# Weights' sign in a Prelu, sums of squares as 128x32 tiles, loads in pairs of chunks: one change to a chunked scan with two gated MLPs

## The chip, the core and the metric

The kernel runs on one core of a Trainium2 chip. A core has TensorE (PE; its weight loads are listed as PEld), VectorE (DVE), ScalarE (ACT), GpSimd (POOL) and SyncE (SP, which issues transfers); each takes its own instructions in order, and they meet at semaphores. The metric is the time of one execution on the device in microseconds (us).

## The reference, cut to what matters

Three stages follow each other. The first is a decayed linear attention over chunks (4 batches, 8 heads, 768 positions, head size 32, state size 16), the second a gated MLP behind an RMS norm, the third an MLP with a hard gate.

```python
# per chunk of 32 positions, per batch and head
cum = np.cumsum(log(clip(a)))
M = (C @ B.T) * exp(cum[:, None] - cum[None, :]) * causal
y = M @ x + (C @ state) * exp(cum)[:, None]
state = exp(sum(la)) * state + (B * exp(cum[-1] - cum)[:, None]).T @ x
# 3072 tokens, width 256 = heads x head size
xn = x / sqrt(mean(x * x) + 1e-6) * rms_g
x = (silu(xn @ w_gate) * (xn @ w_val)) @ w_out      # d_ff 1536
h = x @ w_in                                        # d_ff 2048
out = (h * clip(h + 3, 0, 6) / 6) @ w_out2
```

The weights arrive as 64-bit floats and are turned into 32-bit ones on the chip; the other inputs are 32-bit.

## The kernel before, in words

**Tiling.** The 24 attention chunks (6 blocks of 128 positions by 4 batches, all heads together; `k` counts them) are worked two at a time. For a chunk the kernel loads `cb` (B, C and x in three layouts, 448 KB), `L` (the decay factors of 64 positions, broadcast to the partitions, 256 KB in two transfers) and `P` (prefix products, 64 KB). A scan on VectorE turns `L` into decays, PE makes scores (L395) and state terms (L406), VectorE multiplies by the decays (`SM`, L449), and PE adds the parts within (L420) and from the state (L429). Four chunks make a block of 512 tokens. ScalarE squares them (`sq`), and `norm` (L581) sums the squares over the width, takes 1/sqrt by a bit trick and three Newton steps on VectorE (L519 to L521), writes the 512 results to DRAM (`rnd`, L601), reads them back broadcast to 128 partitions (`rb`, L605), and scales the block with them (L609). The first block has its own form, `norm_pair` (L526), which goes over PE instead of DRAM.

**The MLPs.** The first MLP ("A") takes 6 blocks by 12 slices `f` of d_ff; a step is two hidden products of 6 matmuls each and one output product of 6 (every product in three parts, high and low halves of both operands, `mm3`, L716). The second ("B") takes 6 blocks by 16 slices, with 6 and 6 matmuls. A step goes PE, ScalarE (gate `p`, L751 or L753), VectorE (product `p`, L759 or L761), ScalarE (`gh`), VectorE or GpSimd (`gl`), PE. Only two buffers hold hidden products of A, so PE cannot go far ahead of the product `p` on VectorE.

**Weights.** For each slice, `weights` (L648) loads 64-bit words, ScalarE scales the high words by a Copy (`high`, L664) and the low words (`low`, L668), VectorE joins them by a shift and an or (`join`, L672) and puts the sign bit in (`sign`, L677), and two more operations split the result into high and low halves. There are 12 slices for A and 16 for B.

**What sets the order.** A list scheduler in Python, `Plan` (L38), gets every operation with an estimated cost, its inputs and outputs and a priority, simulates the engines, and writes the instructions in the order in which its simulation starts them. `visit` puts two attention chunks between MLP steps, at slices AT = [1, 5] of every block of A, and `norm` of the next block stands at slice AT_NORM = 7. All transfers are issued by SyncE in the order of the plan. After the last attention chunk, at `open2`, the buffers of the attention are given back and the weights of B are prepared.

Of the kernel before, what the change touches and what calls it, by code (L numbers as in the profile page):

```python
# [17 lines left out]
CH = 128  # L18
# [10 lines left out]
RAW = [17500, 12000]  # L29
BOOST = 6000  # L30
PACE = 0.9
AT = [1, 5]
AT_NORM = 7
NL = 3
NCB = 4


class Plan:  # L38
# [10 lines left out]
    LAT = {"PE": 250, "ACT": 150, "DVE": 130, "POOL": 150, "DMA": 2000, "HOST": 0}  # L49

    def __init__(self, bufs):
        self.bufs, self.ops = bufs, []
        self.last, self.readers, self.users, self.first = {}, {}, {}, {}
        self.fill, self.pace = None, {}

    def op(self, ns, fn, r=(), w=(), boost=0):

        i, deps, order = len(self.ops), set(), set()
        for k in r:
            deps.add(self.last[k])  # L60
        for k in w:
# [19 lines left out]
    def run(self):  # L81
# [8 lines left out]
        for i in reversed(range(len(ops))):  # L90
            ns = ops[i][0]
            e = min(ns, key=ns.get)
            tail[i] = ns[e] + max((tail[s] + (self.LAT[e] if full else 0)
# [9 lines left out]
        done, left, out = set(), set(), []  # L103

# [7 lines left out]
        while len(out) < len(ops):  # L112
# [39 lines left out]
            free[e] = end  # L152
            out.append((t, i, e))
            for s, full in succ[i]:
                ready[s] = max(ready[s], end + self.LAT[e] if full else t)
                wait[s] -= 1
                if wait[s] == 0:
                    enter(s)
# [18 lines left out]
def block_kernel(ctx, tc, comb, ablk, w1, w2, cst, out):  # L177
# [18 lines left out]
    ap3 = att.enter_context(tc.tile_pool(name="ap3", bufs=NL))  # L196
    apc = att.enter_context(tc.tile_pool(name="apc", bufs=NCB))
# [4 lines left out]
    ones = ap1.tile([128, 1], F32, name="ones")  # L202
# [5 lines left out]
    P = Plan({"L": NL, "cb": NCB, "P": NCB, "ch": 4, "bh": 2, "SM": 4, "um": 4, "V": 6, "V1": 4,  # L208
# [9 lines left out]
    def dma(nbytes):  # L218
        return {"DMA": max(500, nbytes // 300)}
# [4 lines left out]
    def d1(n):  # L224
        return 65 + 1.05 * n
# [26 lines left out]
    def setup():  # L252
# [3 lines left out]
        act.activation(out=spare, in_=half, func=AF.Sqrt)  # L256
# [15 lines left out]
    rnd = dram.tile([NB, B * CH], F32, name="rnd")  # L272
# [16 lines left out]
    def put_pref(e):  # L289
        for c in range(2):  # L290
            nc.sync.dma_start(
                out=pref.rearrange("k (q g c i) -> c (k q) g i", q=2, c=2, i=SC)[c],
                in_=ac[48 * c:48 * c + 48])

    def prefixes():
        P.op(dma(98304), lambda e: nc.sync.dma_start(out=ac, in_=rows(ablk)), w=[("ac", 0)],
             boost=1e5)
        P.op({"DVE": d2(256) + 200}, clip_all, r=[("ac", 0), ("eye", 0)], w=[("az", 0)], boost=1e5)
        P.op({"DVE": ds(256)}, prefix, r=[("az", 0)], w=[("ac", 0)], boost=1e5)
        P.op(dma(98304), put_pref, r=[("ac", 0)], w=[("pref", 0)], boost=1e5)  # L300
        P.op(dma(98304), lambda e: nc.sync.dma_start(out=gs, in_=cst), w=[("cs", 0)], boost=2e4)
        P.op(dma(98304), lambda e: nc.sync.dma_start(out=rows(azero), in_=az), r=[("az", 0)],
             w=[("azero", 0)], boost=2e5)

# [25 lines left out]
    def load(k):  # L330
        bst = BOOST if k >= B else BOOST0 + (3000 if k < 2 else 0)

        def ld_cb(e, a, b):
            if ("cb", k) not in T:
                T["cb", k] = apc.tile([128, CW], F32, tag="cb", name="cb")
            nc.sync.dma_start(out=T["cb", k][:, a:b], in_=comb[k][:, a:b])

        def ld_L(e):
            T["L", k] = t = ap3.tile([128, H, SC], F32, tag="L", name="L")
            src = azero if k else ablk  # L340
            for c in range(2):
                nc.sync.dma_start(out=flat(t[64 * c:64 * c + 64]),
                                  in_=src[c, k].partition_broadcast(SC))

        def ld_P(e):
            T["P", k] = t = apc.tile([128, CH], F32, tag="P", name="P")
            src = pref[k].rearrange("(h n i) -> h n i", n=1, i=CH).to_broadcast([H, N, CH])
            nc.sync.dma_start(out=t, in_=src)

        def clip(e):  # L350
            t = T["L", k]
            eng[e].tensor_scalar(out=t, in0=t, scalar1=1e-6, scalar2=1.0, op0=ALU.max, op1=ALU.min)
            eng[e].memset(t[:, :, 0:1], 0.0)

        if k == 0:
            P.op(dma(262144), ld_L, w=[("L", k)], boost=1e5)
            prefixes()
            P.op({"DVE": d1(512)}, clip, r=[("L", k)], w=[("L", k)], boost=bst)
        else:
            P.op(dma(262144), ld_L, r=[("azero", 0)], w=[("L", k)], boost=bst)  # L360
        if k < B:
            P.op(dma(262144), lambda e: ld_cb(e, 0, XX), w=[("cb", k, 0)], boost=bst)
            P.op(dma(196608), lambda e: ld_cb(e, XX, CW), w=[("cb", k, 1)], boost=bst)
        else:
            P.op(dma(458752), lambda e: ld_cb(e, 0, CW), w=[("cb", k, 0), ("cb", k, 1)], boost=bst)
        P.op(dma(65536), ld_P, r=[("pref", 0)], w=[("P", k)], boost=bst)


        def scan(e):
# [4 lines left out]
        P.op({"DVE": ds(512)}, scan, r=[("eye", 0), ("L", k)], w=[("L", k)], boost=bst)  # L374

        def ch(e):
# [4 lines left out]
        def bh(e):  # L381
# [4 lines left out]
        P.op(either(128), bh, r=[("cb", k, 1), ("L", k)], w=[("bh", k)], boost=bst)  # L386
# [566 lines left out]
```

## Time and profile before

| | us |
|---|---|
| median of 3 runs | 711.05 (709.69 to 711.46) |
| the profiled execution: its own time | 709.71 |
| the profiled execution: its span | 707.9 |
| PE busy | 627.9 (89% of the span) |
| VectorE busy | 328.4 (46%) |
| ScalarE busy | 292.9 (41%) |
| GpSimd busy | 263.7 (37%) |
| first matmul of the MLP starts at | 36.68 |
| last instruction's chain: PE on lines 718 | 35% and 26% of the span |
| the same chain: DMA `rnd`, DMA `rb` | 7% and 3% of the span |

PE's busy share is high, but its records overlap, so the share alone doesn't tell how near PE is to its rate; the spacing of the matmuls does. The span begins and ends with stretches in which PE waits or does small work, and between them lie five waits of several us that the timeline of PE shows by themselves. From about 411 us on, PE works without a gap to the end.

### The profile page before, as it was taken

How to read it: one execution, taken by the hardware profiler on the slowest of the kernel's cores; microseconds unless marked ns; L12 is line 12 of the kernel's file. 1: busy time of each engine (PE TensorE's matmuls, PEld its weight loads, DVE VectorE, ACT ScalarE, POOL GpSimd, SP SyncE). 2: the span in 40 equal slices, each digit the busy share in tenths (PEclk: the TensorE clock that was granted, in tenths of full speed). 3: DMA queues.
4: the chain of work that ended last, by engine and by line, in shares of the span. 5: the costliest groups of instructions: out<-in, count | busy, mean ns of one | idle time of the engine just before them, and what ended most of it. 6: DMA issues, size and time to landing. Idle time of an engine off the chain costs nothing.

```text
span 707.9 us, 10946 instructions
## 1 busy us (share of the span) xinstructions
PE 627.9 (89%) x4414; PEld 508.5 (72%) x4414; DVE 328.4 (46%) x518; ACT 292.9 (41%) x483; POOL 263.7 (37%) x228
## 2 busy tenths in 40 slices
PE   2587968994999499959779999999999999999997
PEld 1465757783878387748668778888888888888886
DVE  4699956562156215523258894232233322332323
ACT  1465623321332133223145663545545445454453
POOL 2155423221332122212123434555455545554443
PEclk9998988998999799979979999999999999999999
DMA  7916711230023004100132430000000000000000
GB/s 204 353 62 196 260 20 38 91 91 15 1 91 90 16 0 118 42 15 2 10 125 97 143 120 0 1 1 0 31 1 30 1 0 31 1 30 1 18 12 30
DMA packets 21089, 42.18 MB, mean 60 GB/s; under 512 B 5360, under 2 KB 9136, under 8 KB 21040
## 3 DMA queue, kind: packets, MB, share of 16 engines
q1 hardware_dynamic: 21040, 41.50, 18.7%
q8 instruction: 34, 0.56, 0.4%
q14 instruction: 15, 0.12, 0.1%
HBM read 38.14 MB, written 3.35 MB: 59 GB/s over the span
## 4 chain that ended last, share of the span: by engine, by line
PE 65%; DMA 12%; DVE 10%; issue 5%; ACT 2%; POOL 1%; SPq 0%; DVEq 0%; POOLq 0%; ACTq 0%
PE hps L718 35%; PE acc L718 26%; DMA rnd<-y 7%; DMA rb<-rnd 3%; DMA L<-azero 2%; DVE p L759 1%; DVE cv L677 1%; PE sps L429 1%; PE sps L420 1%; DVE cv L672 1%; DVE z L520 1%; ACT p L751 1%; DVE L L371 1%; DVE gl L240 1%; DVE xT L609 1%
## 5 line engine op out<-in xcount | busy, mean ns | idle before, releaser
L240 POOL TENSOR_TENSOR gl<-p,gh 128x512 fp32r<-128x512 f32 x150 | 196.9, 1313 | 283.2 <-ACT gh L766 274.4
L766 ACT CAST gh<-p 128x512 fp32r<-128x512 f32 x168 | 104.6, 623 | 118.9 <-PE acc L718 116.8
L761 DVE SCALAR_TENSOR_TENSOR p<-p,hps 128x512 f32<-128x512 f32 x96 | 65.9, 687 | 171.3 <-ACT p L753 171.2
L718 PE MATMUL hps<-xh,w1h 128*128 128x512 f32 x288 | 97.6, 421 | 53.6 <-DVE p L759 42.4
L718 PEld LDWEIGHTS hps<-xh,w1h 128*128 128x128 f32 x288 | 54.3, 198 | 71.6 <-DVE p L759 46.5
L753 ACT ACTIVATE p<-hps,half 128x512 f32<-128x512 f32 x96 | 66.0, 688 | 81.5 <-POOL gl L240 80.5
L718 PE MATMUL hps<-xh,w1l 128*128 128x512 f32 x288 | 93.1, 406 | 0.9 <-POOL w1l L240 0.9
L718 PE MATMUL hps<-xl,w1h 128*128 128x512 f32 x288 | 92.8, 405 | 0.0
L759 DVE TENSOR_TENSOR p<-p,hps 128x512 f32<-128x512 f32 x72 | 49.0, 681 | 65.4 <-PE hps L718 60.9
L751 ACT ACTIVATE p<-hps 128x512 f32<-128x512 f32 x72 | 43.0, 597 | 80.7 <-POOL gl L240 54.8
L718 PE MATMUL acc<-gl,w2h 128*128 128x512 f32 x192 | 74.7, 389 | 0.0
L718 PE MATMUL acc<-gh,w2h 128*128 128x512 f32 x192 | 74.7, 389 | 0.0
L718 PE MATMUL acc<-gh,w2l 128*128 128x512 f32 x192 | 74.7, 389 | 0.0
L718 PEld LDWEIGHTS hps<-xh,w1l 128*128 128x128 f32 x288 | 56.8, 197 | 14.0 <-POOL w1l L240 1.3
L718 PEld LDWEIGHTS hps<-xl,w1h 128*128 128x128 f32 x288 | 56.6, 197 | 12.6
L718 PE MATMUL hps<-xl,w2h 128*128 128x512 f32 x192 | 59.1, 389 | 0.0
L718 PE MATMUL hps<-xh,w2h 128*128 128x512 f32 x192 | 59.1, 389 | 0.0
L718 PE MATMUL hps<-xh,w2l 128*128 128x512 f32 x192 | 59.1, 389 | 0.0
L718 PE MATMUL acc<-gh,w1h 128*128 128x512 f32 x144 | 57.6, 400 | 0.0
L718 PE MATMUL acc<-gh,w1l 128*128 128x512 f32 x144 | 56.9, 395 | 0.0
L718 PE MATMUL acc<-gl,w1h 128*128 128x512 f32 x144 | 56.6, 393 | 0.0
L718 PEld LDWEIGHTS acc<-gh,w2l 128*128 128x128 f32 x192 | 36.1, 188 | 7.5
(99 smaller groups left out, 748.3 us busy)
## 6 DMA issues: line engine op xcount, KB each, us to landing
cb<-comb SPq DMA_DIRECT2D x20, 448.0 KB
raw<-w SPq DMA_DIRECT2D x16, 512.0 KB
L<-azero SPq DMA_DIRECT2D x46, 128.0 KB
yT<-w SPq DMA_DIRECT2D x6, 768.0 KB
rawx<-w SPq DMA_DIRECT2D x6, 768.0 KB
out<-yT SPq DMA_DIRECT2D x12, 256.0 KB
P<-pref SPq DMA_DIRECT2D x24, 64.0 KB
rb<-rnd SPq DMA_DIRECT2D x5, 256.0 KB
```

The lines of the kernel that those rows point to most:

```text
L240: eng[e].tensor_tensor(out=out, in0=a, in1=b, op=op)
L371: dve.tensor_tensor_scan(out=L, data0=L, data1=flat(eye8), initial=0.0, op0=ALU.mult, op1=ALU.add)
L420: pe.matmul(out=y[32 * g:32 * g + 32, 2 * t + c], rhs=SM[r, h], lhsT=cb[r, XX + D * h:XX + D * h + D], start=first, stop=True, skip_group_ ...
L429: pe.matmul(out=y[q:q + 64, p // 2 * 2 + c], lhsT=before(k, c)[r, :], rhs=T["ch", k][r, SC * c:SC * c + SC], start=False, stop=True, skip_ ...
L520: dve.tensor_tensor(out=z, in0=z, in1=y, op=ALU.mult)
L609: dve.scalar_tensor_tensor(out=x, in0=x, scalar=gs[:, t:t + 1], in1=T["rb", j], op0=ALU.mult, op1=ALU.mult)
L718: pe.matmul(out=o, lhsT=a, rhs=c, start=first and i == 0, stop=last and i == len(seq) - 1)
L751: act.activation(out=p[:, :n], in_=hid(hs[0])[:, :n], func=AF.Silu)
L753: act.activation(out=p[:, :n], in_=hid(hs[0])[:, :n], func=AF.Relu, scale=1.0 / 6.0, bias=half)
L759: dve.tensor_tensor(out=p, in0=p, in1=h, op=ALU.mult)
L761: dve.scalar_tensor_tensor(out=p, in0=p, scalar=1.0, in1=h, op0=ALU.min, op1=ALU.mult)
L766: act.copy(out=t[:, :n], in_=T["p", i][:, :n])
```

## The change

The diff does five things.

1. **Sign.** `high` uses Prelu with scale 2^-112 and alpha -2^32 in place of Copy. A negative word comes out positive with an exponent that is 32 higher, and the shift by 3 in `join` carries that bit into the sign. `sign` (28 VectorE operations, 12 of 128x768 and 16 of 128x512) is gone.
2. **Norm.** For the blocks 1 to 5 the sums of squares are made with a 128x32 tile of ones as the stationary operand, so that each batch's sums lie along 128 columns, repeated on 32 partitions. The VectorE chain (shift, guess, 3 Newton steps, 12 operations) works on 128x128 elements instead of 128x4. `rnd` is written by 4 transfers of one row of 128 numbers each; it was one transfer that took 4 numbers from each of 128 partitions.
3. **Loads in pairs.** `L`, `cb` and `P` are tiles of two chunks, two such tiles each (before: 3, 4 and 4 tiles of one chunk). A pair's `cb` is one transfer, from the second pair on, and a pair's `L` two transfers with 4 KB rows.
4. **ScalarE issues** the first two pairs' `cb` and the constants `gs`; the table load for Sqrt comes behind the first of these. New order constraints (`seq`) put the second pair's loads and the first weights behind the prefix products, and the third pair behind the third slice of weights.
5. **The planner** gets other costs: transfers have a rate and a landing time, a GpSimd operation delays VectorE by 0.45 of its length. The slices for `visit` and `norm` become [2, 6, 8] for block 0 and [0, 5, 6] for the others.

```diff
-AT = [1, 5]
-AT_NORM = 7
-NL = 3
-NCB = 4
+AT = [[2, 6, 8]] + [[0, 5, 6]] * 4
...
+    RATE, LAND, SHARE = 300, 1700, 0.45
...
+            if e == "POOL":
+                free["DVE"] = max(free["DVE"], t) + self.SHARE * ops[i][0][e]
+            land = end + self.LAT[e]
+            if i in self.bytes:
+                pipe = max(pipe, end) + self.bytes[i] / self.RATE
+                land = pipe + self.LAND
...
-    P = Plan({"L": NL, "cb": NCB, "P": NCB, "ch": 4, "bh": 2, "SM": 4, "um": 4, "V": 6, "V1": 4,
+    P = Plan({"L": 2, "cb": 2, "P": 2, "ch": 4, "bh": 2, "SM": 4, "um": 4, "V": 6, "V1": 4,
...
+        def ld_cb2(e):
+            (act if e == "ACT" else nc.sync).dma_start(
+                out=tile2("cb", q, [CW]), in_=comb[k0:k0 + 2].rearrange("k p m -> p k m"))
...
+        seq = {1: [("P", 0)], 2: [("raw", 2)]}.get(q, [])
...
+            for i in range(2):
+                P.op(dma(458752, 1, "ACT"), lambda e, i=i: ld_cb(e, i), w=[cbs[i]], boost=8e5)
...
         def total(e):
-            for k in range(k0, k0 + B):
-                mean(k)
+            for t in range(2):
+                for i in range(B):
+                    pe.matmul(out=sums()[32 * i:32 * i + 32], lhsT=ones,
+                              rhs=T["sq", j][:, t, i * CH:i * CH + CH],
+                              start=t == 0, stop=t == 1, skip_group_check=True)
...
         def put(e):
-            nc.sync.dma_start(out=rnd[j].rearrange("(c i) -> i c", i=CH), in_=rn(j)[1])
+            for i in range(B):
+                nc.sync.dma_start(out=rnd[j, i:i + 1], in_=rn(j)[1][32 * i:32 * i + 1])
...
-            act.activation(out=T[kt], in_=T[kr][:, :, 1], func=AF.Copy, scale=2.0 ** -112)
+            act.activation(out=T[kt], in_=T[kr][:, :, 1], func=AF.Prelu, scale=2.0 ** -112,
+                           alpha=-2.0 ** 32)
...
-        def sign(e):
-            u = T[kt].bitcast(I32)
-            dve.scalar_tensor_tensor(out=u, in0=T[kr].bitcast(I32)[:, :, 1], scalar=-0x80000000,
-                                     in1=u, op0=ALU.bitwise_and, op1=ALU.bitwise_or)
...
-            P.op({"DVE": d1(cols)}, sign, r=[kr, kt], w=[kt], boost=bst)
...
-            if f in AT:
-                visit((j + 1) * B // 2 + 1 + AT.index(f))
-            if f == AT_NORM:
+            if f in AT[j][:2]:
+                visit((j + 1) * B // 2 + 1 + AT[j].index(f))
+            if f == AT[j][2]:
```

VectorE at the second use of `norm` (block 2), before, from the last Newton operation to the next products `p` (`xT<-xT,gs,rb` is the scaling that waits for `rb`, `xl` and `gl` are low halves):

```order
L521 SCALAR_TENSOR_TENSOR y0_1668<-z0_1669,y0_1668 128x4
L371 SCALAR_TENSOR_TENSOR L_1648<-L_1648,eye8_120 128x512
L759 TENSOR_TENSOR p_1713<-p_1713,hps_1706 128x512
L609 SCALAR_TENSOR_TENSOR xT_1397<-xT_1397,gs_116,rb_1722 128x512 x2
L759 TENSOR_TENSOR p_1742<-p_1742,hps_1735 128x512
L240 TENSOR_TENSOR xl_1753<-xT_1397,xh_1752 128x512
L240 TENSOR_TENSOR gl_1768<-p_1663,gh_1765 128x512
```

The same place after the change:

```order
L552 SCALAR_TENSOR_TENSOR y1_1579<-z1_1580,y1_1579 128x128
L793 TENSOR_TENSOR p_1610<-p_1610,hps_1601 128x512
L400 SCALAR_TENSOR_TENSOR L_1549<-L_1549,eye8_114 128x512 x2
L793 TENSOR_TENSOR p_1653<-p_1653,hps_1644 128x512
L648 SCALAR_TENSOR_TENSOR xT_1318<-xT_1318,gs_110,rb_1651 128x512 x2
L254 CAST xh_1683<-xT_1318 128x512
L248 TENSOR_TENSOR xl_1684<-xT_1318,xh_1683 128x512
L793 TENSOR_TENSOR p_1692<-p_1692,hps_1674 128x512
```

One product `p` stood between the last Newton operation and the scaling, and another between the Newton steps; now two stand between the chain's end and the scaling.

SyncE's issues at the start, before, from the constants on (`yT` and `rawx` are the buffers that take the raw weights):

```order
L301 DMA gs_116<-cst 128x66
L336 DMA cb_156<-comb 128x384
L336 DMA cb_187<-comb 128x512
L342 DMA L_201<-azero_126 64x512 x2
L348 DMA P_206<-pref_125 128x1x128
L348 DMA P_208<-pref_125 128x1x128
L342 DMA L_210<-azero_126 64x512 x2
L342 DMA L_222<-azero_126 64x512 x2
L655 DMA yT_67<-w1 128x1536
L336 DMA cb_273<-comb 128x512
L336 DMA cb_187<-comb 128x384
L336 DMA cb_273<-comb 128x384
```

After the change, from the first load on:

```order
L374 DMA ac_122<-ablk 96x256
L355 DMA L_145<-ablk 64x1024 x2
L302 DMA azero_120<-az_123 96x256
L297 DMA pref_119<-ac_122 192x1x64 x2
L694 DMA yT_67<-w1 128x1536
L364 DMA P_181<-pref_119 128x1x128 x2
L355 DMA L_195<-azero_120 64x1024 x2
L364 DMA P_214<-pref_119 128x1x128 x2
L694 DMA yT_67<-w1 128x1536 x2
L349 DMA cb_288<-comb 128x2x896
```

The halves of `cb_187` and `cb_273` (the third and fourth chunk) stood around the first weights (`yT`); on SyncE no `cb` of the first two pairs is left.

ScalarE at the start, after the change (before, it began with the table load):

```order
L345 DMA cb_143<-comb 128x896 x2
L379 DMA gs_110<-cst 128x66
L381 ACT_TABLE_LOAD
L381 ACTIVATE spare_111<-half_66 128x1
L349 DMA cb_198<-comb 128x2x896
L703 ACTIVATE yT_67<-yT_67 128x768
```

The second pair's `cb` is now the fourth load that ScalarE issues, in one piece. The program has two table loads before and after.

## Rows read from the trace of the kernel before

**Rows 1.** The page's first line: span of the profiled execution.

```profile
span 707.9 us, 10946 instructions
```

**Rows 2.** Timeline of PE: start, us, engine line op; [idle before <- what ended it].

```profile
108.17 0.80 PE L718 MATMUL hps<-xh,w1h 128*128 128x512 f32 x1 [6.14 <-ACT p L751]
...
173.26 0.80 PE L718 MATMUL hps<-xh,w1h 128*128 128x512 f32 x1 [9.11 <-DVE p L759]
...
241.44 0.79 PE L718 MATMUL hps<-xh,w1h 128*128 128x512 f32 x1 [9.28 <-DVE p L759]
...
309.40 0.80 PE L718 MATMUL hps<-xh,w1h 128*128 128x512 f32 x1 [9.42 <-DVE p L759]
...
357.94 0.79 PE L718 MATMUL hps<-xh,w1h 128*128 128x512 f32 x1 [7.97 <-DVE p L759]
```

**Rows 3.** Timeline of VectorE and SyncE in one of the five waits.

```profile
157.08 0.16 DVE L521 SCALAR_TENSOR_TENSOR y<-z,y 128x4 f32<-128x4 f32 x1
...
157.27 0.38 SPq L601 DMA_DIRECT2D rnd<-y  x1
...
158.30 0.66 DVE L759 TENSOR_TENSOR p<-p,hps 128x512 f32<-128x512 f32 x1
...
166.17 0.33 SPq L605 DMA_DIRECT2D rb<-rnd  x1
171.19 1.42 DVE L609 SCALAR_TENSOR_TENSOR xT<-xT,gs,rb 128x512 f32<-128x512 f32 x2 [12.23 <-DMA rb<-rnd]
```

**Rows 4.** Pieces of the chain that ended last: start, us, what.

```profile
148.72 3.20 DMA L<-azero
...
173.26 2.93 PE hps L718 x6
...
177.60 2.72 PE hps L718 x12
...
293.12 11.04 DMA rnd<-y
304.18 3.13 DMA rb<-rnd
...
357.94 7.14 PE hps L718 x18
```

**Rows 5.** DMA packets between 157 and 166 us, under the first of Rows 3's transfers.

```profile
DMA packets 528, 0.00 MB, mean 0 GB/s; under 512 B 528, under 2 KB 528, under 8 KB 528
```

**Rows 6.** Stretches: length, busy PE, PEld, DVE, ACT, POOL; PEclk, DMA share, GB/s.

```profile
10.00:20.00 10.00, 4.44 (x117) 3.03 (x117) 5.40 (x8) 1.37 (x5) 1.55 (x3) 1.00 0.89 260
...
36.60:108.17 71.57, 54.54 (x571) 41.67 (x570) 63.40 (x80) 36.54 (x57) 35.16 (x28) 0.90 0.39 127
...
357.94:411.00 53.06, 51.70 (x210) 40.85 (x210) 41.94 (x53) 31.02 (x54) 19.89 (x15) 0.94 0.31 104
```

**Rows 7.** Groups of VectorE instructions: xcount | busy us, mean ns | idle before.

```profile
L677 DVE SCALAR_TENSOR_TENSOR yT<-yT 128x768 int32<-128x768 int32 x6 | 8.0, 1334 | 0.1
...
L677 DVE SCALAR_TENSOR_TENSOR yT<-rawx,yT 128x768 int32<-128x768 int32 x6 | 7.2, 1192 | 0.1
...
L455 DVE TENSOR_TENSOR um<-sps,gs 128x128 f32<-128x128 f32 x20 | 5.7, 284 | 6.6 <-ACT sq L490 1.4 <-PE sps L406 1.3 <-PE sps L506 1.3
```

**Rows 8.** Timeline of the start, to the first matmul of the MLP.

```profile
4.00 0.43 SPq L302 DMA_DIRECT2D azero<-az  x1
...
7.91 0.48 SPq L342 DMA_DIRECT2D L<-azero  x1
...
20.86 0.41 POOL L240 TENSOR_TENSOR bh<-cb,L 128x128 f32<-128x128 f32 x1 [0.24 <-DMA cb<-comb]
...
36.68 0.77 PE L718 MATMUL hps<-xh,w1h 128*128 128x512 f32 x1
```

**Rows 9.** Groups of PE instructions between 108 and 173 us.

```profile
L506 PE MATMUL sps<-ones,sq 128*128 128x1 f32 x16 | 1.9, 248 | 0.0
...
L395 PE MATMUL sps<-cb 32*64 32x128 f32 x64 | 1.4, 280 | 0.0
```

More of the change, by code (lines that the diff above doesn't have):

```diff
@@ L53, in __init__, with op @@
         self.last, self.readers, self.users, self.first = {}, {}, {}, {}
-        self.fill, self.pace = None, {}
-    def op(self, ns, fn, r=(), w=(), boost=0):
+        self.fill, self.pace, self.bytes = None, {}, {}
+    def op(self, ns, fn, r=(), w=(), boost=0, seq=()):
         i, deps, order = len(self.ops), set(), set()
+        ns = dict(ns)
+        if "bytes" in ns:
+            self.bytes[i] = ns.pop("bytes")
         for k in r:
             deps.add(self.last[k])
+        for k in seq:
+            order.add(self.last[k])
         for k in w:
@@ L92, in run @@
             e = min(ns, key=ns.get)
-            tail[i] = ns[e] + max((tail[s] + (self.LAT[e] if full else 0)
+            more = self.bytes[i] / self.RATE + self.LAND if i in self.bytes else self.LAT[e]
+            tail[i] = ns[e] + max((tail[s] + (more if full else 0)
                                    for s, full in succ[i]), default=0)
@@ new lines, in load @@
+        if q == 0:
+            P.op(dma(98304), lambda e: nc.sync.dma_start(out=ac, in_=rows(ablk)), w=[("ac", 0)],
+                 boost=1e6)
+            P.op(dma(524288, 2), ld_L, w=Ls, boost=9e5)
+            for i in range(2):
+                P.op(dma(458752, 1, "ACT"), lambda e, i=i: ld_cb(e, i), w=[cbs[i]], boost=8e5)
+            P.op(dma(33792, 1, "ACT"), lambda e: act.dma_start(out=gs, in_=cst), w=[("cs", 0)],
+                 boost=7e5)
+            P.op({"ACT": 1500}, lambda e: act.activation(out=spare, in_=half, func=AF.Sqrt),
+                 w=[("table", 0)], boost=5e5)
@@ L832, in block_kernel @@
         norm_pair(q, 0)
-    P.op({"ACT": 1400}, lambda e: act.activation(out=spare, in_=half, func=AF.Silu),
-         r=[("rn", 0, q, 2) for q in range(2)], w=[("table", 0)], boost=BOOST0)
+    P.op({"ACT": 1500}, lambda e: act.activation(out=spare, in_=half, func=AF.Silu),
+         r=[("rn", 0, q, 2) for q in range(2)], w=[("table", 0)], boost=1e6)
     xkeys[0] = [("x", 0, q, u) for q in range(2) for u in range(2)]
@@ L846, in visit @@
         r, w = [], []
-        for k in new:
-            load(k)
+        if new:
+            load(q)
         for k in new:
```

155 lines of the change are left out of this document (82 added, 73 removed).

## The prediction, made before the changed kernel was timed

> **What bounds the kernel now.** I read the page first, then PE's timeline, then who is late at each of its waits. The span is 707.9 us [rows 1]; the profiled execution took 709.71, so 1.8 us lie around the span, and the median of the runs, 711.05, is 1.3 above it. PE is the engine that matters: when it isn't kept waiting, 12 matmuls take 2.72 us [rows 4], 0.227 us each. There are 6 x 12 x 18 + 6 x 16 x 12 = 2448 of them, so the MLPs alone are 555 us. What can be won is the rest, and it sits in three places: a start in which PE has no MLP work until 36.68 us [rows 8], the first block, in which VectorE is busy 63.4 of 71.6 us [rows 6], and five waits of 6.14, 9.11, 9.28, 9.42 and 7.97 us, 41.9 together [rows 2].
>
> The five waits are one pattern. PE waits for the product `p`; `p` stands in VectorE's queue behind the scaling L609, which waited 12.23 us for `rb` [rows 3]. The round trip over DRAM is what is late: the write of `rnd` was issued at 157.27, the read at 166.17, and the scaling began at 171.19, so 8.9 and 5.0 us, 13.9 in all. In another block it is 11.04 and 3.13 [rows 4], the same sum: when the write is told later, the read takes less. So most of it is one thing that drains, and the read by itself is about 3.1 us; a read of the same 256 KB for `L` took 3.20 [rows 4]. After each wait PE also runs slow for a while: the first 6 matmuls after the second wait take 2.93 us where 6 fast ones take 1.36, and the 18 after the last one 7.14 against 4.08 [rows 4].
>
> **The change part by part.**
>
> *The round trip (takes most away).* The write consists of 528 packets, all under 512 B [rows 5]: 512 single numbers and 16 for the semaphore. They are replaced by 4 transfers of one row of 512 B. No such write is in the trace. Its bounds: the four issues cost 4 x 0.38 = 1.5 us on SyncE [rows 3], the last begins 1.14 after the first; from there to landing at least 2 us is my estimate (3.20 us for a read with two issues [rows 4], less one issue and a microsecond for its bytes), at most 3.9 (the 96 KB write of `azero`, issued at 4.00 in full traffic, had landed when its reader was issued at 7.91 [rows 8]). So the write takes 3.1 to 5.0 us, and I take 3.2, since traffic is low there. The read then takes 3.1 (up to 5.0 if its length is its own). Sum 6.3, bounds 6.2 and 10, in place of 13.9.
>
> The Trainium skill ("DMA: Bandwidth & Descriptors", Why a DMA increments its semaphore by 16 and not by 1) says that a transfer is split over the engines by its slowest dimension, which could cut each row of 128 numbers into 16 pieces of 32 B. As an estimate from that, 64 small packets drain in an eighth of the present time, 1 to 1.4 us more for each block, and the wait left in each block would be near 1.0 in place of 0.5 us, and the sum below would give about 642. No row shows it.
>
> What covers 6.3 us? Call the end of the Newton chain T. Before, the last `p` ahead of the scaling started at 158.30, 1.1 us behind T [rows 3], and PE ran dry at 173.26 - 9.11 = 164.15 [rows 2], 5.85 us after the start of that `p`. After the change two products stand between T and the scaling. A step of the first MLP is 18 matmuls, 4.08 us, so the second of them starts near T + 4.2 and PE runs dry near T + 10. `rb` is there at T + 6.3; two scalings (1.42 [rows 3]), a cast and a low half (estimate 1.3) later the next `p` starts at T + 9.0 and ends at 9.7. That just fits; I leave 0.5 us for each of the five blocks. Waits that short leave no slow stretch. Slow stretches now cost 2.93 - 1.36 = 1.57 after each of the first four waits and 7.14 - 4.08 = 3.06 after the last: 9.3. **Gain 41.9 + 9.3 - 2.5 = 48.7**, bounds 25 (round trip of 10 us: about 3 us of wait and 1.6 of slow matmuls stay in each block) and 51.
>
> What it costs: the Newton chain works on 128 columns. The nearest row, a 128x128 product, takes 0.284 us [rows 7], the small operations 0.16 [rows 3]; 12 operations are 1.5 us longer. That lies on the chain to `rb`, but ahead of T, where PE still has the work of an earlier `p`; the chain of 3.4 us fits inside the 4.08 us of a step. SyncE's next loads stand behind the four issues, 1.1 us later than before; nobody waits for them.
>
> *The sums of squares.* 16 PE records, 1.9 us in each block [rows 9], become 8 products of 32 columns that may lie side by side. Nearest: 64 records of 32x64 tiles take 1.4 us [rows 9], 0.35 for 16. Between 0.35 and 1.9 I take 0.9. **Gain 5 x 1.0 = 5**, bounds 0 and 7.5; this is PE time.
>
> *The sign.* Twelve operations of 8.0 + 7.2 = 15.2 us leave VectorE in the first block [rows 7]. Between 36.6 and 108.17 PE was idle 71.57 - 54.54 = 17.0 us, 6.1 of which is the norm's wait, so 10.9 others, and the mean clock was 0.90 [rows 6], so a few us more went into slow matmuls. With a quarter of VectorE's work gone, most of these waits should close, not all: ScalarE and GpSimd still make the halves. I leave 4 us and count no clock. **Gain 7 to 13, taken as 10.** Bounds: 0 if another engine is late next, 13 if all close. Prelu in place of Copy on ScalarE I take at the same price (the order shows two table loads before and after). In the second MLP's preparation PE idled 53.06 - 51.70 = 1.4 us [rows 6]; the sixteen signs there lie beside busy PE, and I count nothing.
>
> *The start.* The second pair's last `cb` was in use at 20.86 [rows 8], and 15.8 us later came the first matmul. After the change the loads that the second pair needs, and all that stand ahead of them, are about 4.1 MB (two pairs of `cb` 1.8, two of `L` 1.0, one slice of weights 0.8, the rest 0.5). At the 260 GB/s of the second 10 us [rows 6] that is 16 us, so with a start near 2 the data is there at 15 to 18 in place of 20.9. The chain behind it is the same length, with one sign less. First matmul at 30.7: **gain 6**, bounds 0 and 9.
>
> *The planner's other costs and the new slices* move visits by one or two steps. No row prices that; since every visit's loads have at least 5 steps of 4.08 us to arrive, I take zero, from -2 to +2.
>
> **Sum:** 48.7 + 5 + 10 + 6 = 69.7; 709.7 - 69.7 = 640.0. Against the whole: now 707.9 - 36.7 - 555 - 41.9 - 9.3 - 10.9 = 54 us are left for the attention's matmuls, the tail and small waits; in the forecast it is 640 - 1.8 - 30.7 - 555 - 2.5 - 0.9 = 49, less by the 5 of the sums of squares. So the floor is not crossed. If the median stands to the profiled time as it does now, it is 0 to 1.3 more. **Forecast 640.**
>
> **The rivals.**
>
> *A, start bounded by bytes.* In 10 to 20 us the DMA engines were busy 0.89 of the time [rows 6], and ScalarE's loads move the same bytes over them. If the second pair's `cb` on the second queue only takes turns with `L` and the weights, the first matmul stays at 36.7 and the time is 640 + 6 = 646. The Trainium skill says so ("DMA: Bandwidth & Descriptors", Issuing engines are not separate DMA queues): issue from several engines saves only the time of the issue. By that rule, rival A's time. Against it: the order of the bytes changes too, two slices of weights move behind the second pair.
>
> *B, the round trip stays long.* If a DRAM write is told only after several us whatever its packets, or the read keeps its 5 us, the trip is 10 us and 24 of the gain are lost: 664. For it: no row shows a small write of whole rows. Against it: the constant sum.
>
> *C, VectorE was not what held the first block.* If the cover is gone and ScalarE or GpSimd is late next, the 10 us stay: 650.
>
> *D, slower: loads of pairs come late.* A pair's tile comes free only when both chunks of the pair two before are done, so a pair's 1.57 MB are loaded between two visits, 5 steps (20.4 us) or 7 (28.6). At 260 GB/s that is 6 us, well covered. If the loads took x us, ten visits would wait 10x - 245 in sum; that eats the gain of 70 from x = 31.5 on (50 GB/s). At 45 GB/s x is 35, 105 us are lost, and the time is 745. The 260 GB/s of the start speak against it.
>
> **How the numbers follow.** Chances: forecast 0.56 (own range 628 to 650), A 0.12, B 0.14, C 0.12, D 0.03, several failing together 0.03 (664 to 712, of which 0.02 within 0.3%). The low end takes start, sums and first block at their best: 640 - 3 - 2.5 - 3 - 2.5 = 629, and 2 for the visits, 627. The high end is B, 664. Since 0.3% is about what a measurement of this kernel can tell from no change: faster 0.95, same 0.02, slower 0.03.
>
> **What would show it.** Right: PE's five waits of 6 to 9 us gone or under 2; `rnd` issue to `rb` issue near 3.2 us and to the scaling near 6.3; no VectorE line for signs; L622 near 0.9 us for each block; the first MLP matmul near 31; blocks 2 to 4 some 12 us shorter each. Wrong: a scaling that still waits over 5 us for `rb`; first matmul after 35; waits of PE for score tiles behind `cb`; more than two table loads; a Prelu that takes longer than the Copy did.

## The result, and the profile after

The changed kernel takes 643.36 us (median of 4 runs, 642.86 to 644.16), the kernel before, run beside it, 710.55: a ratio of 0.9055 (95% interval 0.9039 to 0.9071), 67 us less. The forecast was 640.0. The profiled execution of the changed kernel took 643.43 with a span of 641.6, so 1.8 us lie around the span as before, and the two spans [rows 1] differ by 66.3 us.

The page of the changed kernel: the span, the busy time of the engines, and the granted clock of PE in 40 slices.

```profile
span 641.6 us, 10828 instructions
...
PE 608.3 (95%) x4414; PEld 491.9 (77%) x4414; DVE 311.2 (49%) x474; ACT 293.9 (46%) x484; POOL 282.1 (44%) x245
...
PEclk9999999999999999999999999999999999999999
```

PE is busy 95% of the span, and no slice shows a granted clock under nine tenths of full speed; the mean granted clock is 0.999 of full speed, and was 0.961 before. The chain that ended last shows the round trip of the second norm, which answers [rows 3, 4] (start us, us, what):

```profile
130.42 0.45 DVE y L552
130.89 0.27 SPq L640
...
131.78 1.08 DMA rnd<-y
...
133.01 3.25 DMA rb<-rnd
136.28 2.05 DVE xT L648 x2
```

The first of four writes is issued at 130.89, the read at 133.01, and the scaling starts at 136.28: 2.1 + 3.3 = 5.4 us where the kernel before took 13.9. Over the five norms the trip is 5.0 to 6.8 us, before 13.9 to 14.9. The five waits of PE [rows 2] are gone: behind the first block, in what is left of the first MLP the longest idle pieces of PE are 0.47 and 0.60 us. Two stretches of the trace after, from the first MLP matmul to 108 us, which is the first block and a little more, and the blocks behind it (columns as in [rows 6]):

```profile
37.05:108.00 70.95, 68.24 (x807) 53.36 (x807) 60.72 (x85) 41.84 (x69) 36.59 (x32) 1.00 0.45 153
...
108.00:357.00 249.00, 245.35 (x2071) 197.51 (x2070) 143.23 (x224) 102.17 (x182) 100.13 (x89) 1.00 0.23 71
```

In the first of them PE idles 70.95 - 68.24 = 2.7 us, before 17.0 [rows 6], and its clock there went from 0.90 to 1.00. Three groups answer [rows 7, 9]: the sums of squares, the Prelu, and the join on VectorE, the only operation there that is left for a weight's bits (one of its two groups).

```profile
L622 PE MATMUL sps<-sq,ones 128*32 128x128 f32 x80 | 3.2, 279 | 0.1
...
L703 ACT ACTIVATE yT<-rawx 128x768 f32<-128x768 f32 x6 | 5.4, 902 | 0.7 <-DVE w1l L248 0.7
...
L712 DVE SCALAR_TENSOR_TENSOR yT<-yT 128x768 int32<-128x768 int32 x6 | 7.2, 1206 | 0.0
```

The sums cost 3.2 us in all five blocks, 0.64 each in place of 1.9. The Prelu takes 902 ns; the Copy in its place took 909.

Summed over both traces, the 66.3 us came from here: PE's idle time behind its first MLP matmul 56.2 to 8.5 us, 47.7; MLP matmuls that follow each other slowly (spacings over 350 ns, counted above 227) 17.4 to 3.9, 13.5; the rest of PE's work 39.0 to 33.4, 5.6; and the start, 36.68 to 37.05, gave 0.4 back. **Two places gained nothing: the start, and the second MLP, which even got longer.** Timeline of the start (start us, us, engine line op; [idle before <- what ended it]):

```profile
8.83 0.89 DVE L368 TENSOR_SCALAR L<-L 128x512 f32<-128x512 f32 x2 [3.58 <-DMA L<-ablk]
...
11.35 1.34 SPq L364 DMA_DIRECT2D P<-pref  x2
12.80 1.14 SPq L355 DMA_DIRECT2D L<-azero  x2
...
17.80 2.34 DVE L400 TENSOR_TENSOR_SCAN L<-L,eye 128x512 f32<-128x512 f32 x2 [1.13 <-DMA L<-azero]
...
20.87 1.81 POOL L248 TENSOR_TENSOR w1l<-yT,w1h 128x768 fp32r<-128x768 f32 x1 [6.11 <-ACT w1h L252]
22.64 0.78 POOL L248 TENSOR_TENSOR bh<-cb,L 128x128 f32<-128x128 f32 x2
...
37.05 1.20 PE L752 MATMUL hps<-xh,w1h 128*128 128x512 f32 x2
```

The second pair's last data is there at 17.80, 3.1 us sooner than the 20.86 of [rows 8]; but then come two scans, and the two `bh` stand on GpSimd behind the first `w1l`. From the data to the first matmul it is 19.2 us, before 15.8. The data could have come sooner still: the second pair's `L` was issued at 12.80, in the kernel before at 7.91 [rows 8], since the new constraint puts it behind the prefix products, whose transfer `pref`, issued at 5.99, held SyncE until 11.35.

From its first matmul (`hps<-xh,w2h`) to its last, the second MLP takes 273.07 us; before, without a gap, it took 269.44. At the start of a block VectorE's low half `xl` now stands ahead of the product `p` that PE waits for:

```profile
407.57 1.60 DVE L248 TENSOR_TENSOR xl<-yT,xh 128x512 fp32r<-128x512 f32 x1
...
409.10 0.67 DVE L795 SCALAR_TENSOR_TENSOR p<-p,hps 128x512 f32<-128x512 f32 x1
...
409.82 0.73 PE L752 MATMUL hps<-xh,w2h 128*128 128x512 f32 x2 [0.36 <-DVE p L795]
```

The sums above hold these 3.6 us as a loss.

### The profile page after: what moved, and what is told of

The parts are those of the page before. It is cut to its first block, busy times and chain, and to the rows that moved or that the text cites. A ratio compares the mean times of both kernels' runs of the same rounds, so it can differ in the third digit from the quotient of the medians.

```text
span 641.6 us, 10828 instructions
## 1 busy us (share of the span) xinstructions
PE 608.3 (95%) x4414; PEld 491.9 (77%) x4414; DVE 311.2 (49%) x474; ACT 293.9 (46%) x484; POOL 282.1 (44%) x245
## 4 chain that ended last, share of the span: by engine, by line
PE 78%; DVE 11%; DMA 5%; issue 4%; SPq 1%; ACT 0%; POOL 0%; DVEq 0%; POOLq 0%
PE hps L752 43%; PE acc L752 31%; DMA rb<-rnd 2%; DVE p L793 1%; DVE z L551 1%; DVE xT L648 1%; PE sps L451 1%; PE sps L460 1%; DVE xl L248 1%; DVE xh L254 1%; DVE yT L712 1%; DMA pref<-ac 1%; PE sps L426 1%; DVE y L552 1%; DMA rnd<-y 1%
## 5 line engine op out<-in xcount | busy, mean ns | idle before, releaser
L248 POOL TENSOR_TENSOR gl<-p,gh 128x512 fp32r<-128x512 f32 x161 | 215.5, 1338 | 300.0 <-ACT gh L800 279.7
L752 PE MATMUL hps<-xh,w1h 128*128 128x512 f32 x288 | 91.2, 398 | 4.4 <-DVE p L793 3.7
L752 PE MATMUL hps<-xh,w1l 128*128 128x512 f32 x288 | 89.4, 392 | 0.0
L752 PE MATMUL hps<-xl,w1h 128*128 128x512 f32 x288 | 89.2, 391 | 0.0
L752 PEld LDWEIGHTS hps<-xh,w1h 128*128 128x128 f32 x288 | 53.1, 190 | 19.2 <-DVE p L793 6.8
L752 PEld LDWEIGHTS hps<-xh,w1l 128*128 128x128 f32 x288 | 54.4, 189 | 11.7
L752 PEld LDWEIGHTS hps<-xl,w1h 128*128 128x128 f32 x288 | 54.4, 189 | 11.6
L752 PEld LDWEIGHTS hps<-xh,w2h 128*128 128x128 f32 x192 | 35.6, 188 | 11.3 <-DVE p L795 4.3
```

Of the source, the lines that this page charges most:

```text
L248: eng[e].tensor_tensor(out=out, in0=a, in1=b, op=op)
L752: pe.matmul(out=o, lhsT=a, rhs=c, start=first and i == 0, stop=last and i == len(seq) - 1)
```

## The experiments

Runs of one group share a chip and the runs of the kernel before, whose median was 711.67 in the first group (round trip, sign, order), 711.38 in the second, 714.55 in the third and 707.55 in the last. Between groups a difference of half a per cent says little, so ratios or the traces are used there.

### The round trip: how small are the pieces?

*Pieces of 4 bytes again* (e1_put4b):

```
-for i in range(B):
-    nc.sync.dma_start(out=rnd[j, i:i + 1], in_=rn(j)[1][32 * i:32 * i + 1])
+for b in range(2):
+    nc.sync.dma_start(out=rnd[j][:, b::2], in_=rn(j)[1][0:128:32, b::2])
```

> The changed kernel with one edit: the normaliser's 4 x 128 numbers are again written to DRAM in pieces of 4 bytes (two DMAs with every second column, 4 partitions each, 512 pieces), and read as in the changed kernel. Nothing else differs. Theory (the trip was long because of the 512 small pieces): the stretch from the last Newton operation to the landing of rb goes from 5.4 us back to 13 to 15 us, a wait of 6 to 9 us comes back in front of each of the five blocks with slow matmuls behind it, 643.4 + 35 to 50 = 678 to 693 us. Rival (the trip was long because its source lay as 4 numbers in each of 128 partitions, or it became short through the planner, not through the size of the pieces): the trip stays at 5 to 7 us and the time at 642 to 648 us.

Measured: 690.71 us, 47 more than the changed kernel; ratio 0.9703 (0.968 to 0.9725). All five waits are back, 7.86, 7.89, 7.64, 7.26 and 7.69 us. PE's and VectorE's rows at the second, and the DMA engines' busy tenths (40 slices) and packets between the write's issue and the read's, 141.4 to 151.1 us:

```profile
155.84 1.42 DVE L648 SCALAR_TENSOR_TENSOR xT<-xT,gs,rb 128x512 f32<-128x512 f32 x2 [9.99 <-DMA rb<-rnd]
...
157.79 1.22 PE L752 MATMUL hps<-xh,w1h 128*128 128x512 f32 x2 [7.89 <-ACT p L785]
```

```profile
DMA  0000022120000000000000000000000000000000
...
DMA packets 520, 0.00 MB, mean 0 GB/s; under 512 B 520, under 2 KB 520, under 8 KB 520
```

The trip is 155.84 - 141.39 = 14.4 us. But the packets move only in slices 6 to 9 of 40, and from about 143.8 to 151.1 nothing moves: **the write is not slow to be sent, it is told late.** The kernel before shows the same between 157.2 and 166.1, under [rows 5]:

```profile
DMA  0000470000000000000000000000000000000000
```

*Pieces of 16 bytes* (e2_put16b), 128 of them, in two DMAs:

```
+for b in range(2):
+    nc.sync.dma_start(out=rnd[j].rearrange("i (a b c) -> i b a c", b=2, c=4)[:, b],
+                      in_=rn(j)[1][0:128:32].rearrange("i (a b c) -> i b a c", b=2, c=4)[:, b])
```

> The changed kernel with the same write in pieces of 16 bytes (two DMAs, 128 pieces). Theory, if the trip grows with the number of pieces: (13.9 - 5.4) x 128/512 = about 2 us more trip, five waits of 1 to 2 us, 646 to 654 us. Rival, if every write that is not one whole row is slow whatever its count: as with 4 bytes, 678 to 693 us. Third: pieces of 16 bytes cost nothing, 642 to 645 us.

Measured: 643.50 us, nothing lost. Trip 136.90 - 131.25 = 5.6 us. Slices of 131.2 to 133.6, the write's and the read's issue:

```profile
DMA  0000000000000000000002100000001210000000
...
DMA packets 136, 0.00 MB, mean 1 GB/s; under 512 B 136, under 2 KB 136, under 8 KB 136
```

Here the read is issued 0.4 us behind the last packets. This left open whether the count (128 against 512) or the size of a piece decides.

*One row in pieces of 4 bytes* (e7_row4b), 128 of them, the other three rows whole:

```
+for b in range(2):
+    nc.sync.dma_start(out=rnd[j, 0:1, b::2], in_=rn(j)[1][0:1, b::2])
+for i in range(1, B):
+    nc.sync.dma_start(out=rnd[j, i:i + 1], in_=rn(j)[1][32 * i:32 * i + 1])
```

> The changed kernel with one of the four rows written in pieces of 4 bytes (128 pieces, two DMAs), the other three as rows of 512 B. 128 pieces of 16 bytes cost nothing, 512 pieces of 4 bytes 9.1 us from the last issue to the read's issue. If the number of pieces sets it: 1 to 2 us from the last issue to the read, 643 to 645 us. If a piece of 4 bytes is slow each, from the first on (9.1/512 = 18 ns each): 2 to 3.5 us, 643 to 648 us. If any write with such pieces has a fixed long end: 7 to 9 us, 680 to 690 us.

Measured: 679.24 us, ratio 0.9495 (0.9477 to 0.9512); five waits of 5.16 to 5.91 us. Slices of 137.4 to 145.3, and VectorE's wait:

```profile
DMA  0000001001000000000000000000000000000000
```

```profile
149.29 1.41 DVE L650 SCALAR_TENSOR_TENSOR xT<-xT,gs,rb 128x512 f32<-128x512 f32 x2 [7.46 <-DMA rb<-rnd]
```

Trip 149.29 - 137.38 = 11.9 us, with some 5 us of silence behind the last packet. So 128 pieces of 16 bytes cost nothing and 128 of 4 bytes 6.5 us of trip; four times as many cost 2.5 more. The size of the piece decides, most of its price is a fixed end, and of the three cases the third came nearest. Sizes between 4 and 16 bytes weren't tried, and what happens in the silence no record shows.

### The parts, each alone

*The norm alone, on the kernel before* (b1_norm): `norm` with its sums, its chain on 128x128 and its row writes; no other part.

```
-            for k in range(k0, k0 + B):
-                mean(k)
+            for t in range(2):
+                for i in range(B):
+                    pe.matmul(out=sums()[32 * i:32 * i + 32], lhsT=ones,
...
-            nc.sync.dma_start(out=rnd[j].rearrange("(c i) -> i c", i=CH), in_=rn(j)[1])
+            for i in range(B):
+                nc.sync.dma_start(out=rnd[j, i:i + 1], in_=rn(j)[1][32 * i:32 * i + 1])
```

> The kernel before with the norm part of the change alone: sums of squares as 128x32 tiles, the Newton steps on 128x128, the factors written as 4 rows of 512 B. Sign, loads, planner's prices and slices stay as before. Theory (the forecast's two terms, 48.7 for the five waits and 5 for the sums, need nothing of the rest): 710.5 - 54 = 654 to 660 us, no wait over 2 us in front of a block. Rival (part of that gain needs the new slices, which move the norm to slice 8 or 6, or the sign's VectorE time): 660 to 675 us, with waits of 1 to 3 us left in front of the blocks.

Measured: 658.61 us against 711.38, ratio 0.9262 (0.9235 to 0.929), 52.8 us. Up to 108 us, though, PE's idle time fell by less than the norm's wait of 6.14 us there:

```profile
36.87:108.00 71.13, 57.88 (x594) 43.48 (x593) 69.97 (x83) 37.17 (x59) 36.91 (x28) 0.95 0.40 137
```

PE idles 13.25 us, VectorE is busy 69.97 of 71.13: the small waits there grew from 10.9 to 13. So the rival was half right: the forecast's size held, yet waits up to 2.2 us stayed there, 9.1 us of them in all for VectorE's `p`.

*The sign alone, on the kernel before* (b2_sign), and *undone in the changed kernel* (e3_sign):

```
-act.activation(out=T[kt], in_=T[kr][:, :, 1], func=AF.Copy, scale=2.0 ** -112)
+act.activation(out=T[kt], in_=T[kr][:, :, 1], func=AF.Prelu, scale=2.0 ** -112,
+               alpha=-2.0 ** 32)
-P.op({"DVE": d1(cols)}, sign, r=[kr, kt], w=[kt], boost=bst)
```

> The kernel before with Prelu in place of Copy and the sign operation, all else as before. Theory from the run that put the sign back (+5): 704 to 707 us. The forecast's own term (10): 699 to 702 us. Rival (the sign was hidden under the waits of the norm there): 709 to 712 us.

Measured: 701.04 against 711.38, 10.3 us, ratio 0.9853 (0.9821 to 0.9885): the forecast's term, not the smaller one. By the traces (9.3 us between the two profiled executions) 1.5 of it lies in the start, 5.0 in the first block and 2.7 in the last block of the first MLP, where the second MLP's weights are prepared.

> The changed kernel with the sign undone: Copy on ScalarE and the separate sign operation on VectorE for all 28 weight tiles, the planner told so. Theory (VectorE held block 0): 12 sign operations of 0.95 us and more come back on VectorE between 37 and 108 us, PE's waits there go from 1.9 back to 8 to 11 us with 2 to 4 us of slow matmuls, 652 to 658 us. Rival (block 0's gain came from the planner's new costs and the moved slices, VectorE has room): 642 to 646 us.

Measured: 648.37 us, 4.9 more than the 16-byte run of the same group, which runs like the changed kernel. But the time is the sum of two opposite differences. The second MLP starts at 373.27 us in place of the changed kernel's 364.79, 8.5 later, and then takes 269.71 us in place of 273.07: with the sign put back the planner happens to make an order without the waits shown above. So up to the second MLP the sign is worth 8.5 us here, not half of what it is worth on the kernel before.

*Both parts, on the kernel before* (b3_both): no new loads, no new prices, old slices.

> The kernel before with the norm part and Prelu, with its own loads, planner's prices and slices. If the parts add up as they did alone (-52 and -10): 647 to 650 us, and the new loads, prices and slices are worth the 4 to 6 us that are left to the changed kernel. Rival (the sign's VectorE time is what was left of block 0's waits, the rest is worth nothing): 642 to 645 us.

Measured: 646.75 us, ratio 0.9036 (0.9016 to 0.9057). By time that is additive and 3.4 above the changed kernel; by ratio it is the changed kernel's own 0.9055. Which of the two can't be settled by the times. The traces say more: its second MLP starts at 372.24 us, 7.4 later than in the changed kernel, and takes 269.44 us, 3.6 less. So the new loads, prices and slices give 7.4 us and take 3.6 back.

*Old slices and old prices for VectorE in the changed kernel* (e6_plan); the new costs of transfers stay:

```
-AT = [[2, 6, 8]] + [[0, 5, 6]] * 4
+AT = [[1, 5, 7]] * 5
...
-    RATE, LAND, SHARE = 300, 1700, 0.45
+    RATE, LAND, SHARE = 300, 1700, 0
...
-        return 72 + 1.04 * n
+        return 65 + 1.05 * n
```

> The changed kernel with the planner's old table of slices (1, 5, 7 in every block) and its old prices for VectorE (65 + 1.05 n, no share for GpSimd's operations). No operation is added or taken away, only their order moves. Theory (order worth 0 within 2): 641 to 646 us. Rival (the gain in block 0 is the order's): 648 to 656 us with PE waits of 6 us and more in block 0.

Measured: 645.45 us, 2.0 more than the 16-byte run of its group, the edge of what the theory allowed. Again two differences cancel: the second MLP starts at 370.18 us, 5.4 later than in the changed kernel, and takes 269.44 us, 3.6 less. Only the order differs, so the new order is worth 5.4 us in the first MLP and costs 3.6 in the second. From the first MLP matmul to 108 us in the three kernels b3_both, e3_sign and e6_plan, in this order:

```profile
35.72:108.00 72.28, 65.68 (x638) 50.80 (x638) 60.88 (x87) 41.18 (x65) 35.79 (x30) 0.98 0.43 144
```

```profile
37.93:108.00 70.07, 65.13 (x633) 49.05 (x633) 66.42 (x86) 40.49 (x65) 38.08 (x31) 1.00 0.39 130
```

```profile
37.74:108.00 70.26, 63.82 (x633) 49.23 (x633) 62.11 (x87) 39.11 (x61) 39.17 (x30) 1.00 0.42 140
```

With the new norm in all of them, PE idles to 108 us (length less PE's busy time); behind it, how long the first 216 MLP matmuls take, which are one block:

| | loads and order of before | loads and order of after |
|---|---|---|
| with the sign on VectorE | 13.25, block 77.0 (b1_norm) | 4.9, block 66.7 (e3_sign) |
| without it | 6.6, block 67.8 (b3_both) | 2.7, block 61.1 (after) |

e6_plan, without the sign and with the new loads but the old order, idles 6.4 us and takes 67.0 us for the block, like b3_both: of loads and order it is the order that counts here. The same waits can be closed from either side: by taking work off VectorE, or by an order that puts VectorE's work where it holds nobody. Either remedy is worth less when the other is there: the sign 9.2 us of the block in the old order and 5.6 in the new one.

### The start: what keeps the first MLP matmul at 37 us?

*The second pair's `cb` later* (s1_cb). ScalarE's early issue is dropped; SP issues it behind the second pair's `L`; the planner's order of everything else stays.

```
-P.op(dma(917504, 1, "ACT"), ld_cb2, w=cbs, boost=6e5, seq=[Ls[0]])
+P.op(dma(917504, 1, "ACT"), lambda e: None, w=cbs, boost=6e5, seq=[Ls[0]])
 ...
                     .partition_broadcast(SC))
+            if q == 1:
+                ld_cb2("DMA")
```

> The changed kernel with one load moved: the second pair's cb is issued by SP behind the second pair's L instead of by ScalarE at 2.2 us; the planner's order of all other work is kept. Theory A (the early ScalarE load takes the first pair's L bytes and time from it; the start is bound by when data comes): L is clipped at 5.5 to 6.5 us instead of 8.8, and the first matmul of the MLP comes at 33.5 to 35.5 us instead of 37.05, 640 to 642 us. Theory B (the order of work behind the data sets the start): L earlier all the same, but the first matmul of the MLP moves by under 1 us, 642.5 to 644 us.

Measured: 643.64 us, no change. Timeline:

```profile
8.93 0.89 DVE L370 TENSOR_SCALAR L<-L 128x512 f32<-128x512 f32 x2 [3.56 <-DMA L<-ablk]
...
16.69 2.33 DVE L402 TENSOR_TENSOR_SCAN L<-L,eye 128x512 f32<-128x512 f32 x2
...
22.75 0.78 POOL L248 TENSOR_TENSOR bh<-cb,L 128x128 f32<-128x128 f32 x2
...
37.15 1.20 PE L754 MATMUL hps<-xh,w1h 128*128 128x512 f32 x2
```

Theory A falls: the first pair's `L` comes no sooner (8.93), so the early `cb` did not hold it. What it did hold is `pref`, 3.24 us here and 5.31 in the changed kernel (chain, start us, us; the changed kernel first). So the second pair's `L` comes sooner, VectorE's scans no longer wait for it, and still `bh` runs at 22.75, behind `w1l`.

```profile
5.99 5.31 DMA pref<-ac
```

```profile
6.10 3.24 DMA pref<-ac
```

*Order on PE and GpSimd* (s2_order): the second pair's scores ahead of the first pair's means, `w1l` behind `bh`.

```
-    norm_pair(0, 0)
+    norm_pair(0, 0, [place(3) + (0, 1)])
...
-        P.op(either(cols), lo, r=[kt if wide else kr, kh], w=[kl], boost=bst)
+        P.op(either(cols), lo, r=[kt if wide else kr, kh], w=[kl], boost=bst,
+             seq=[("bh", 3)] if not tag and f == 0 else ())
```

> The changed kernel with two places of its order changed in the start: the second pair's scores stand ahead of the first pair's means on PE, and GpSimd's first w1l stands behind the second pair's bh. Theory B: the second pair's state matmuls at 21 to 22.5 us instead of 23.5, the first matmul of the MLP at 35 to 36.3 us instead of 37.05, 641 to 642.7 us. Theory A (data comes too late for order to matter): the first matmul of the MLP stays within 0.5 us of 37.05, 643 to 644 us.

Measured: 642.41 us, ratio 0.9034 (0.9009 to 0.9059 holds the changed kernel's 0.9055). `bh` came at 19.70 in place of 22.64, the first MLP matmul at 37.45: nothing of the 3 us arrived. Beside s1_cb of the same group, which runs like the changed kernel, it takes 1.2 us less, and no run of the one reaches the other's; that came behind the start, where PE idles 1.7 us to 108 us in place of 2.7.

*Both, and more of the order* (s3_all): the edits of s1_cb and s2_order, and the first pair's `xl` and the first two `w1l` held on GpSimd, the second weight tile's `w1l` and join behind the second pair's Newton steps.

```
+        P.op({"POOL": g1(cols)} if not tag and f < 2 else either(cols), lo,
+             r=[kt if wide else kr, kh], w=[kl], boost=bst,
+             seq=[("bh", 3) if f == 0 else ("rn", 0, 1, 1)] if not tag and f < 2 else ())
...
+            P.op({"DVE": d1(cols)}, join, r=[kr + (0,), kt], w=[kt], boost=bst,
+                 seq=[("rn", 0, 1, 1)] if not tag and f == 1 else ())
```

> The changed kernel with the start in another order: the second pair's cb issued by SP behind its L, the second pair's scores ahead of the first pair's means on PE, GpSimd's first two w1l and VectorE's join of the second weight tile behind the work of the second pair that they stood ahead of, the first pair's xl on GpSimd. Theory (behind the second pair's data the order of work on GpSimd, VectorE and PE sets the start): second pair's state matmuls at 20.5 to 22 us, first matmul of the MLP at 34 to 36 us instead of 37.05, 639 to 642 us. Rival (the chain of the first pair, whose L is clipped at 8.8 to 9.5 us, sets when the second can follow): second pair's matmuls come sooner but the first matmul of the MLP stays at 36.5 to 37.5 us.

Measured: 647.57 us, ratio 0.9053 (0.9034 to 0.9072), no better than the changed kernel by either. In its trace the start did get shorter:

```profile
17.80 1.16 PE L428 MATMUL sps<-cb 32*64 32x128 f32 x32 [1.01 <-DMA cb<-comb]
...
30.62 1.23 PE L576 MATMUL sps<-eye,y 128*128 128x128 f32 x4 [1.89 <-DVE y L554]
...
34.11 2.23 DVE L248 TENSOR_TENSOR xl<-xT,xh 128x512 fp32r<-128x512 f32 x1
...
35.45 1.20 PE L758 MATMUL hps<-xh,w1h 128*128 128x512 f32 x2
```

The second pair's norm ends 2.9 us sooner (30.62, in the changed kernel 33.50), the first MLP matmul 1.6. But the planner made another order of the first block, and up to 108 us PE idles 72.55 - 66.55 = 6.0 us in place of 2.7: the gain was lost. So the last run kept the order behind the start.

*The start alone* (s6_best): the same places moved, the second weight tile's three steps put into idle time, the planner's order kept from the first MLP matmul on. A step is planned where it was, but written out behind another one:

```
+    def move(key, fn, anchor):
+        def plain(e):
+            moved.setdefault(key, lambda: fn(e))
+            if anchor in done:
+                run(key)
+        return plain
...
+        lo_ = move("lo0", lo, "bh3") if not tag and f == 0 else lo
```

> The changed kernel with the planner's order kept from the first matmul of the MLP on, and only these moved in the start: the second pair's cb issued by SP behind its L; half of the second pair's scores ahead of the first pair's means on PE; GpSimd's first w1l behind the second pair's bh; VectorE's ch of the second pair behind its SM; the second weight tile's three steps (ScalarE's second half, VectorE's join, ScalarE's w1h) earlier, into idle time of these engines, so that the join no longer stands ahead of the second pair's Newton steps. The last reordering of the start brought the second pair's Newton result 2.9 us forward, but the planner made another order of block 0 that took the gain back, so here the order behind is kept. Theory (the order of work behind the data sets the start): the second pair's result (eye matmuls) at 30.5 to 31.8 us instead of 33.5, first matmul of the MLP at 34 to 35.5 us instead of 37.05, block 0's waits as in the changed kernel, 640 to 642 us. Rival (the data sets it): first matmul at 36.5 to 37.5 us, 643 to 644 us.

Measured: 643.15 us (641.53 to 643.86), ratio 0.9092 (0.9077 to 0.9107), first MLP matmul at 36.75. The rival's numbers; by time it is the changed kernel's, by ratio a little worse. Four rows show where it went:

```profile
18.45 0.73 PE L447 MATMUL sps<-cb 32*64 32x128 f32 x16 [1.48 <-DMA cb<-comb]
...
31.13 1.80 POOL L261 TENSOR_TENSOR w1l<-yT,w1h 128x768 fp32r<-128x768 f32 x1
...
31.22 1.73 DVE L586 TENSOR_TENSOR z<-z,y 128x2 f32<-128x2 f32 x1
...
33.20 1.22 PE L611 MATMUL sps<-eye,y 128*128 128x128 f32 x4 [2.95 <-DVE y L587]
```

With `cb` moved back, `cb` is now the last data (18.45; in s3_all 17.80), and a Newton operation of 0.16 us took 1.73 beside GpSimd's `w1l`, which now runs at that moment: it ended at 32.95, the `w1l` at 32.93. Where something waits for it, the second pair's data is complete at 17.8 to 18.5 whichever of its loads is sent first, and every order behind it found a next wait. No run shows one step that sets the first MLP matmul. Loading the first pair's `L` chunk by chunk wasn't tried; no version of the start was found that clearly beats the changed kernel's.

## Why the prediction was right, point by point

**The round trip: right, and better than its bounds.** Forecast 3.2 + 3.1 us, measured 2.1 + 3.3. The write lies below my lower bound of 3.1, because the price "from there to landing at least 2 us" was taken from a read; from the last issue to the read's issue it is 1.2 us (131.78 to 133.01). Norm and sums alone were forecast at 53.7 and gave 52.8 (b1_norm). The reading "most of it is one thing that drains" was half right: the constant sum did belong to the write, and 4-byte pieces alone bring it back (e1_put4b), but the packets are gone after 2 us or so and the rest is silence. Rival B is excluded.

By the rule of the Trainium skill ("DMA: Bandwidth & Descriptors", Why a DMA increments its semaphore by 16 and not by 1) the rows could have been cut into pieces of 32 B; for a contiguous row it says that software can split it so. The trace doesn't show such a split: between 130.9 and 133.0 us only 8 packets moved, 4 of them rows of 512 B:

```profile
DMA packets 8, 0.00 MB, mean 1 GB/s; under 512 B 4, under 2 KB 8, under 8 KB 8
```

It would not have mattered, since pieces of 16 B cost nothing.

**The sums of squares:** 0.9 us forecast, 0.64 measured, a gain of 6.3 in place of 5.

**The sign:** 10 forecast, 10.3 measured on the kernel before, but not where I had put it: by the traces 5.0 lay in the first block, 1.5 in the start (first MLP matmul at 35.19; two of the twelve operations stand there) and 2.7 in the preparation of the second MLP, for which I had counted nothing. That the sum met the forecast is luck. With the norm's waits gone the first block alone gave 9.2 (b1_norm to b3_both), so the mechanism holds there. "I leave 4" of the 10.9 us of waits: 2.7 were left, and the clock of that block rose as well, of which I had counted nothing. Rival C, that the ten would stay, is excluded; a part of them, though, could have been had by order alone.

**The planner and the slices:** zero within 2; e6_plan says 2.0. This is luck too: it is 5.4 us won in the first MLP less 3.6 lost in the second, and the reason I gave, that every visit's loads have time to arrive, prices neither. What the order changed is which operation VectorE does ahead of the product that PE waits for.

**The start: the step that failed.** "The chain behind it is the same length, with one sign less." The data came at 17.8, at the late end of the 15 to 18 I gave, which by itself would have been worth 3 us; I had counted its bytes and left out that its issue waits for `pref`. But before, the last thing to come was a `cb`, with only `bh` left to make of it; now it is `L` for two chunks at once, with 2.34 us of scans ahead of `bh`, and `bh` stood behind `w1l`. The chain is 19.2 us in place of 15.8. That these two make it longer is read off the timeline and not shown: with `bh` 3 us sooner the first matmul did not move (s2_order). The time that rival A gave to the start is what came, the first MLP matmul at 37.05 (its 36.7). Its reason is borne out in part: ScalarE's early `cb` made `pref` 2 us longer. But the data was there 3.1 us sooner than before, and it is the work behind it that ate this. The Trainium skill says that transfers issued by several engines interleave on the same DMA engines ("DMA: Bandwidth & Descriptors", Issuing engines are not separate DMA queues), and s1_cb agrees: with the load moved from ScalarE to SP, SP's `pref` took 3.24 us in place of 5.31.

**Sum.** Forecast 48.7 + 5 + 10 + 6 = 69.7. Measured 66.3: the norm with its slow matmuls, the sums and the first block gave 3 us more than their terms (47.7 + 13.5 + 5.6 = 66.8 against 63.7, with the 3.6 lost in the second MLP taken off), the start 6.4 less. The forecast was 3.4 us low, because the start gave nothing and other errors made up for half of it: that it lies no further off is partly luck, and rival A's 646 is nearer to the measured time.

**Rival D** had no place: no wait for `cb` or `L` is left behind the start.

## What to carry to other kernels

When two small transfers stand between a chain and its user, look at what the queues do between issue and landing: if the packets are gone and nothing moves, the form of the pieces is the thing to change, not the traffic. A remedy for waits on a full engine can be work taken away or a better order; price them together, since each takes a part of the other's gain. When an edit changes a planned order, compare the stages and not the total: here a gain in one stage and a loss in another hid behind 2 us. And when a load is moved forward, follow what becomes the last input instead, and how much work is behind that one.

## What the runs showed of the hardware that I had not expected

- A DRAM write with 4-byte pieces was told complete several us after its last packet had moved, by the issue of the read that waits for it: 6.7 to 7.6 us for 512 pieces (e1_put4b, and the second norm of the kernel before), 4.4 to 5.3 for 128 (e7_row4b). With 128 pieces of 16 bytes or rows of 512 bytes it took 0.3 to 0.6 us. The read that followed was longer too in the second norm, 4.66 us behind 512 pieces, 3.87 behind 128, 3.25 behind rows; but not always, since in the kernel before one took 3.13 [rows 4].
- A VectorE operation can take ten times its time beside GpSimd: 128x2 in 1.73 us in place of 0.16 (s6_best), 128x128 in 1.26 in place of 0.29 (the changed kernel's norm), `xl` in 2.23 in place of 0.67 us (s3_all). Such an operation on a chain is worth more care than its price alone suggests.
